# An attention and gated-MLP kernel: the last sum of x blocks cut in eight steps and set behind the bias additions

## The chip, the cores and the metric

The kernel runs on one core of a Trainium2 chip. The metric is device time in microseconds (us) of one execution; shown is the median of several.

## What is computed

Sigmoid attention for 8 batches of 12 heads, and behind it a gated MLP with a mixing over the sequence:

```python
# q, k, v: (8, 12, 448, 64);  S = 448, d_model = 768, d_ff = 1024
scores = scale * q @ k.T - log(S)
x = sigmoid(scores) @ v              # -> (8, 448, 768)
h = relu(x @ w_in)
u, v = h[..., :512], h[..., 512:]
v_n = (v - mean(v)) / sqrt(var(v) + 1e-6)
v_s = einsum('ts,bsd->btd', w_spatial, v_n) + b_spatial[None, :, None]
out = (u * v_s) @ w_out
```

## The kernel before

All data is float32. A matrix product is made of three products of rounded parts: each operand is kept as a high part and a low part (the rest), in the type fp32r. High parts are copies that ScalarE or VectorE makes, low parts are VectorE subtractions; `split` (lines 121 to 123) does both.

The program runs over four pairs of batches, m = 0 to 3. A pair goes through attention (scores psc, value products pav; x lands in `x_s`, high and low), then the MLP of the pair: `gate_values` (the half v of h: products pv, relu, layer norm into `mlp`) for the seven tiles of 128 rows in the groups (0, 1), (2, 3), (4, 5), (6,); then `spatial`, the mixing, in four blocks of 20 products into PSUM tiles pg, for the two batches b0, b1 and two pairs of feature blocks each; `biased`, which adds the bias to a finished pg on VectorE and puts the result g in SBUF (line 712; the fourth of them goes to `wval_s`); then the half u; then `output`.

For m = 1 to 3 the half u is made by `gated_by_blocks`: block products with seven instead of eight multiplications, as in Strassen's and Winograd's scheme. Blocks of the weights are ready sums in DRAM (`load_block` fetches them one by one on SyncE's queue, w_u_s<-w_u), and blocks of x are summed on VectorE: `x_sums` makes t2, t3 and t4 in a list of 21 steps (a generator, each `yield` one VectorE step, some with a ScalarE copy behind), `x_last_sum` makes t1 in place, in the parts of `x_s` that hold one block of x. `spare(n)` runs the next n steps of the lists in `jobs`, so the calls of `spare` in the layer norm and behind it fix where the steps stand. The seven products come in the order 11 (tiles ua), 21 (ub, first half), t2 (ua), t1 (ub, second half), t3 (ua), t4 (ua), 22 (ub). When 11 is done, ScalarE copies ua into the buffer r1; r1, r2, r3 are the results in SBUF.

PSUM has four buffers (pool ps_2, `bufs=4`) that rotate through pv, pg, ua, ub and po. The four pg take all of them; ua_m_0 takes the buffer of the first pg, ua_m_1 that of the second, ub_m_0 and ub_m_1 those of the third and fourth, each free when `biased` has read it.

At the end `in_program_order` chains each engine's instructions in the order in which the code wrote them, so each queue is fixed by the program text. Semaphores between engines are set by the tiles that instructions share.

Of the kernel before, what the change touches and what calls it, by code (L numbers as in the profile page):

```python
# [8 lines left out]
F32 = mybir.dt.float32  # L9
# [5 lines left out]
P = 128  # L15
# [20 lines left out]
def attn_gmlp_kernel(  # L36
# [25 lines left out]
    nc = tc.nc  # L62
    B, NHP, _, _ = qk.shape
    S = out.shape[3]
# [18 lines left out]
    work = ctx.enter_context(tc.tile_pool(name="work", bufs=2))  # L83
# [8 lines left out]
    KH = NCC // 2  # L92
# [9 lines left out]
    wval_s = const.tile([P, 3 * 512], U32, name="wval_s")  # L102
# [18 lines left out]
    def split(hi, lo, src, copy):  # L121
        copy(hi, src)  # L122
        nc.vector.tensor_sub(lo, src, hi.bitcast(F32))  # L123
# [304 lines left out]
    jobs = []  # L428

    def spare(n):  # L430

        while jobs and n:
            if next(jobs[0], None):
                n -= 1
            else:
                jobs.pop(0)
# [73 lines left out]
    sums = {}  # L510

    def x_part(k, j, ks, a):
        return x_s[:, a, k * KH + ks.start : k * KH + ks.stop, j * S : (j + 1) * S]
# [62 lines left out]

    def x_last_sum(m):

        ks = slice(0, KH)
        t = wval_s[:, : KH * S].bitcast(F32).rearrange("p (k s) -> p k s", k=KH)  # L580
        hi, lo = (x_part(0, 1, ks, a) for a in range(2))
        nc.vector.tensor_add(t, hi.bitcast(F32), lo.bitcast(F32))  # L582
        for a in range(2):
            nc.vector.tensor_sub(t, t, x_part(0, 0, ks, a).bitcast(F32))  # L584
        split(hi, lo, t, nc.scalar.copy)

    def gate_values(m, ts):

        n = len(ts)
        pv = banks(f"pv_{m}_{ts[0]}")  # L590
        for i, t in enumerate(ts):
            product(
                pv[:, i, :F],
                [
                    (
                        lambda a, cc=cc, t=t: x_s[:, a, cc, t * P : (t + 1) * P],
                        lambda c, cc=cc: w_g_s[:, cc, c, :],
                    )
                    for cc in range(NCC)
                ],  # L600
            )
        if n > 1:
            load_weights(1 if ts[0] else 5)
        if not ts[0]:
            spare(8)
        rv = work.tile([P, 2, 512], F32, tag="tmp", name=f"rv_{m}_{ts[0]}", bufs=3)
        nc.scalar.activation(rv[:, :n], pv[:, :n], AF.Relu)
        mv = work.tile([P, 2, 2], F32, tag="mv", name=f"mv_{m}_{ts[0]}")
        for i in range(n):
            stats = work.tile([P, 6], F32, tag="stats", name=f"stats_{m}_{ts[i]}")  # L610
            nc.vector.bn_stats(stats, rv[:, i])  # L611
            nc.vector.bn_aggr(mv[:, i], stats)
        rstd = work.tile([P, 2], F32, tag="rstd", name=f"rstd_{m}_{ts[0]}")
        mean = work.tile([P, 2], F32, tag="mean", name=f"mean_{m}_{ts[0]}")
        nc.gpsimd.tensor_scalar_add(rstd[:, :n], mv[:, :n, 1], 1e-6)
        nc.gpsimd.tensor_tensor(rstd[:, :n], rstd[:, :n], mhalf[:, :n], op=ALU.pow)
        if m:
            nc.vector.tensor_scalar_mul(mean[:, :n], mv[:, :n, 0], -1.0)
            spare(2)
        for i in range(n):  # L620
            if m:
                nc.scalar.activation(rv[:, i], rv[:, i], AF.Identity, bias=mean[:, i : i + 1])
            else:
                nc.vector.tensor_scalar_sub(rv[:, i], rv[:, i], mv[:, i, 0:1])
        load_weights(n - 1)
        for i, t in enumerate(ts):
            vn = slots["tile"][:, t]
            if t != NFULL:
                parts = [(vn[:, 0], vn[:, 1], slice(0, P))]
            else:  # L630

                a, c = slice(0, HALF), slice(HALF, P)
                parts = [(vn[a, 0], vn[c, 0], a), (vn[c, 1], vn[a, 1], c)]
            for hi, lo, rows in parts:
                if m:
                    nc.scalar.activation(  # L636
                        hi, rv[rows, i], AF.Identity, scale=rstd[rows, i : i + 1]
                    )
                else:
                    nc.vector.tensor_scalar_mul(hi, rv[rows, i], rstd[rows, i : i + 1])  # L640
                nc.vector.scalar_tensor_tensor(  # L641
                    lo,
                    rv[rows, i],
                    rstd[rows, i : i + 1],
                    hi.bitcast(F32),
                    op0=ALU.mult,
                    op1=ALU.subtract,
                )
            vns[t] = vn
        if n == 1:  # L650
            load_weights(1)
# [101 lines left out]
    def gated_by_blocks(m):  # L753

        b0, b1 = 2 * m, 2 * m + 1
        x = {
            name: [
                x_s[:, :, k * KH + ks, j * S : (j + 1) * S] for ks in range(KH)
            ]
            for name, k, j in (("11", 0, 0), ("21", 1, 0), ("22", 1, 1), ("t1", 0, 1))  # L760
        }
        x |= sums
        r1, r2 = (work.tile([P, 2, S], F32, tag="v", name=f"ur_{m}_{n}", bufs=2) for n in range(2))
        r3 = work.tile([P, 1024], F32, tag="raw", name=f"ur_{m}_2", bufs=4)[:, : 2 * S].rearrange(
            "p (i s) -> p i s", i=2
        )

        def products(ps, pos, mv, begins, then=None):
            w = block(pos)
            ops = [(a, ks, c) for ks in range(KH) for a, c in TERMS]  # L770
            for i in range(2):
                for n, (a, ks, c) in enumerate(ops):
                    col = (ks * 2 + i) * P
                    nc.tensor.matmul(  # L774
                        ps[i],
                        w[:, a, col : col + P],
                        x[mv][ks][:, c],
                        start=begins and n == 0,
                        stop=n == len(ops) - 1,
                        skip_group_check=True,  # L780
                    )
                if then:
                    then(i)
            if pos + SLOTS_U < NB:
                load_block(pos + SLOTS_U)

        def copied_to(r, ps):
            return lambda i: nc.scalar.copy(r[:, i], ps[i])

        def added_to(r, ps):  # L790
            return lambda i: nc.vector.tensor_add(r[:, i], ps[i], r[:, i])

        pairs = (0, 1), (2, 3)
        pa = [banks(f"ua_{m}_{i}")[:, 0, :S] for i in range(2)]
        products(pa, 0, "11", True, copied_to(r1, pa))
        both = [banks(f"ub_{m}_{i}") for i in range(2)]
        pw, pz = ([ps[:, n, :S] for ps in both] for n in range(2))
        products(pw, 1, "21", True, added_to(r1, pw))
        settle(b0, pairs[0], gates.pop((b0, pairs[0])), r1)
        products(pa, 2, "t2", False, copied_to(r2, pa))  # L800
        products(pz, 3, "t1", True)

        def copied_and_added(i):
            copied_to(r3, pa)(i)
            added_to(r3, pz)(i)

        products(pa, 4, "t3", False, copied_and_added)
        settle(b1, pairs[1], gates.pop((b1, pairs[1])), r3)
        products(pa, 5, "t4", False)
        g = gates.pop((b0, pairs[1]))  # L810
        settle(b0, pairs[1], g, [(g[:, i], pa[i]) for i in range(2)])
        products(pz, 6, "22", False, added_to(r2, pz))
        settle(b1, pairs[0], gates.pop((b1, pairs[0])), r2)
# [260 lines left out]
    for m in range(B // 2):  # L1074
        attention(m)
        slots_of_mlp(m)
        if m:
            jobs.append(x_sums(m))
        for ts in ((0, 1), (2, 3), (4, 5), (6,)):
            gate_values(m, ts)  # L1080
        if m:
            spare(99)
        b0, b1 = 2 * m, 2 * m + 1
        more = m < B // 2 - 1
        for b in (b0, b1):
# [4 lines left out]
        spatial_shorts(m, pairs)  # L1090
        biased(b0, pairs[0])
        if m:
            x_last_sum(m)
        for b, fcs in ((b0, pairs[1]), (b1, pairs[0])):
            spatial(b, fcs)
            biased(b, fcs)
        spatial(b1, pairs[1])
        if m:
            biased(b1, pairs[1])
            gated_by_blocks(m)  # L1100
            start_loads(m + 1)
            if more:
                for pos in range(SLOTS_U):
                    load_block(pos)
            output(b0, (0, 1))
        else:
            gated(b0, pairs[0])
            biased(b1, pairs[1])
            gated(b0, pairs[1])
            gated(b1, pairs[0])  # L1110
            start_loads(m + 1)
            output(b0, (0, 1))
            gated(b1, pairs[1])
            jobs.append(weight_sums())
# [72 lines left out]
```

## Time and profile before

| | |
|---|---|
| median of 3 runs | 664.58 us (662.57 to 664.81) |
| the profiled execution | 663.31 us, of which its span 661.5 us |
| TensorE (PE) busy | 649.5 us, 98% of the span |
| VectorE (DVE) busy | 398.7 us, 60% |
| ScalarE (ACT) busy | 311.1 us, 47% |
| GpSimd (POOL) busy | 27.8 us, 4% |
| mean granted TensorE clock | 0.995 of full |

The profile is of one execution; the span runs from its first to its last instruction. PE is TensorE's product, PEld its weight load, which overlaps it. A row of a timeline merges like instructions that follow each other ("x9") and says in brackets how long the engine stood idle ahead of it and what ended that. Ends of products are modelled, so starts are the safer numbers.

### The profile page before, as it was taken

The page shows a single profiled execution, that of the slowest core. Times are in us where ns is not written, and L with a number is a line of the kernel's source. Part 1 is how long each engine was busy: PE and PEld are TensorE (multiplying, and loading weights), DVE is VectorE, ACT ScalarE, POOL GpSimd, SP SyncE. Part 2 cuts the span into 40 slices and gives each one's busy share as a digit, 9 for nine tenths or more (in the row PEclk, how much of TensorE's full clock was granted, in tenths as well). Part 3 has the DMA queues.
Part 4 walks back from the last instruction along what each step waited for, and adds up shares of the span by engine and source line. Part 5 has one row for each costly group of instructions (what it writes and reads, how often), then busy time and mean ns, then how long its engine had stood idle before and what let it go on. Part 6 is the DMA issues. An engine that isn't in the chain of part 4 may idle for free.

```text
span 661.5 us, 10047 instructions
## 1 busy us (share of the span) xinstructions
PE 649.5 (98%) x4208; PEld 503.5 (76%) x4208; DVE 398.7 (60%) x549; ACT 311.1 (47%) x374; POOL 27.8 (4%) x63
## 2 busy tenths in 40 slices
PE   9999999999999999899999999989999999998997
PEld 3645889999765588799966658879996666887997
DVE  4989889849476386826066637673506754767420
ACT  6986322323777545122178745512218774541221
POOL 0000010000000002000000002100000000210000
PEclk9999999999999999999999999999999999999999
DMA  8764213565872000047544200003944410001213
GB/s 300 262 184 161 63 37 101 161 235 220 317 266 58 1 1 0 1 144 292 196 152 169 58 1 1 1 7 137 316 183 143 169 57 2 0 1 48 96 56 111
DMA packets 25117, 77.85 MB, mean 118 GB/s; under 512 B 2416, under 2 KB 8944, under 8 KB 25072
## 3 DMA queue, kind: packets, MB, share of 16 engines
q1 hardware_dynamic: 24784, 76.98, 33.5%
q8 instruction: 33, 0.54, 0.3%
q10 hardware_dynamic: 288, 0.23, 0.1%
q14 instruction: 12, 0.10, 0.1%
HBM read 60.69 MB, written 16.52 MB: 117 GB/s over the span
## 4 chain that ended last, share of the span: by engine, by line
PE 88%; DVE 8%; ACT 3%; issue 1%; POOL 1%; POOLq 0%
PE po L407 17%; PE pv L407 16%; PE pav L929 15%; PE psc L325 14%; PE ua L774 6%; PE ub L774 5%; PE pav L374 5%; PE pu L407 4%; PE psc L307 3%; PE pg L695 2%; DVE wval_s L584 1%; DVE mlp L641 1%; DVE g L712 1%; DVE stats L611 1%; DVE x_s L123 1%; DVE wval_s L582 1%
## 5 line engine op out<-in xcount | busy, mean ns | idle before, releaser
L407 PE MATMUL pv<-w_g_s,x_s 128*128 128x512 f32 x504 | 115.5, 390 | 0.0
L407 PEld LDWEIGHTS pv<-w_g_s,x_s 128*128 128x128 f32 x504 | 94.3, 188 | 22.3 <-issue 2.1
L289 ACT ACTIVATE ats<-psc,bias_s 128x896 f32<-128x896 f32 x102 | 95.1, 1006 | 19.9 <-PE pav L929 13.5
L325 PEld LDWEIGHTS psc<-qks 64*128 64x128 f32 x840 | 78.1, 185 | 14.8 <-issue 4.9
L325 PE MATMUL psc<-qks 64*128 64x448 f32 x840 | 88.6, 365 | 0.0
L407 PE MATMUL po<-mlp,w_out_s 128*128 128x448 f32 x396 | 82.8, 362 | 0.0
L407 PEld LDWEIGHTS po<-mlp,w_out_s 128*128 128x128 f32 x396 | 74.3, 188 | 4.9
L929 PE MATMUL pav<-ats,v 64*64 64x448 f32 x720 | 76.0, 539 | 0.0
L695 PE MATMUL pg<-w_sp_s,mlp 128*128 128x448 f32 x320 | 65.8, 364 | 0.0
L695 PEld LDWEIGHTS pg<-w_sp_s,mlp 128*128 128x128 f32 x320 | 59.7, 188 | 5.4 <-issue 1.2
L929 PEld LDWEIGHTS pav<-ats,v 64*64 64x64 f32 x720 | 28.3, 133 | 37.3 <-issue 26.6
L842 ACT COPY osb<-po 128x896 f32<-128x896 f32 x23 | 20.8, 906 | 65.2 <-PE po L407 62.1
L275 DVE TENSOR_TENSOR qks<-raw,qks 128x848 fp32r<-128x848 f32 x46 | 47.4, 1041 | 1.0
L123 DVE TENSOR_TENSOR x_s<-pav,x_s 128x896 fp32r<-128x896 f32 x16 | 17.4, 1090 | 50.8 <-ACT x_s L122 50.8
L407 PE MATMUL po<-gs,w_out_s 128*128 128x448 f32 x180 | 39.2, 362 | 0.0
L641 DVE SCALAR_TENSOR_TENSOR mlp<-rv,rstd,mlp 128x512 fp32r<-128x512 f32 (+1 forms) x32 | 23.5, 750 | 22.2 <-ACT mlp L636 21.7
L407 PEld LDWEIGHTS po<-gs,w_out_s 128*128 128x128 f32 x180 | 33.8, 188 | 2.3
L774 PE MATMUL ub<-x_s,w_u_s 128*128 128x448 f32 x162 | 35.4, 373 | 0.0
L268 DVE CAST qks<-raw 128x848 fp32r<-128x848 f32 x38 | 22.7, 597 | 19.3 <-PE po L407 13.1
L774 PEld LDWEIGHTS ub<-x_s,w_u_s 128*128 128x128 f32 x162 | 32.0, 197 | 2.4
L929 PE MATMUL pav<-at,v 64*64 64x448 f32 x216 | 31.9, 536 | 0.0
L901 DVE COPY wval_s<-psc 128x896 f32<-128x896 f32 x9 | 9.8, 1091 | 35.8 <-PE psc L325 35.8
(120 smaller groups left out, 794.4 us busy)
## 6 DMA issues: line engine op xcount, KB each, us to landing
raw<-qk_dram SPq DMA_DIRECT2D x47, 456.0 KB, 4.9
w_u_s<-w_u SPq DMA_DIRECT2D x21, 768.0 KB, 5.7
v<-v_dram SPq DMA_DIRECT2D x24, 448.0 KB, 3.4
out_dram<-osb SPq DMA_DIRECT2D x23, 448.0 KB, 2.6
wraw<-w_in_dram SPq DMA_DIRECT2D x12, 512.0 KB, 5.1
wraw<-w_out_dram SPq DMA_DIRECT2D x6, 512.0 KB, 3.8
w_u<-x_s SPq DMA_DIRECT2D x4, 768.0 KB, 3.6
w_u<-w_u_s SPq DMA_DIRECT2D x3, 768.0 KB, 5.6
```

The lines of the kernel that those rows point to most:

```text
L123: nc.vector.tensor_sub(lo, src, hi.bitcast(F32))
L268: (nc.vector.tensor_copy if b > 1 or halfway else nc.scalar.copy)(s[:, 0], raw)
L275: nc.vector.tensor_sub(s[:, 1], loaded[b, hp][:, HALF:], s[:, 0].bitcast(F32))
L289: nc.scalar.activation(at, src, AF.Sigmoid, bias=bias_s, scale=QK)
L325: nc.tensor.matmul(psc[:, j, :S], st[rows, k : k + P], mv[rows, Q:PART], start=i == 0, stop=i == len(ops) - 1,)
L374: nc.tensor.matmul(pav[heads, odd, :S], vt[rows, t, heads], at[rows, j], start=start, stop=t == NFULL,)
L407: nc.tensor.matmul(ps, st, mv, start=i == 0, stop=i == len(ops) - 1)
L641: nc.vector.scalar_tensor_tensor(lo, rv[rows, i], rstd[rows, i : i + 1], hi.bitcast(F32), op0=ALU.mult, op1=ALU.subtract,)
L695: nc.tensor.matmul(pg[:, i, :S], st, mv, start=n == 0 and not ended, stop=n == len(ops) - 1 and ended,)
L774: nc.tensor.matmul(ps[i], w[:, a, col : col + P], x[mv][ks][:, c], start=begins and n == 0, stop=n == len(ops) - 1, skip_group_check=True,)
L842: nc.scalar.copy(osb, po[:, :, :S])
L929: ins = nc.tensor.matmul(pavs[pair][heads, i % 2, :S], vt[rows, t if t == NFULL else t + i % 2 * (NFULL + 1), heads], at[rows, j], start=i ...
```

## The change

`x_last_sum` becomes a list of steps in `jobs` behind `x_sums`. It works in two halves, of two blocks (896 columns) and of one (448), each of one addition, two subtractions, a ScalarE copy of the high part, and a subtraction of the low part at the end: eight VectorE steps for four. Its scratch is r3 and the first part of r1 instead of `wval_s`; so r1, r2 and r3 are taken there and handed to `gated_by_blocks`. The call `spare(99)`, which ended the other sums ahead of the first bias, is gone; four steps run behind the first bias, three behind the second, three behind the third, the rest behind the fourth. And the layer norm of the tiles (2, 3) and (4, 5) takes three steps instead of two.

```diff
     def x_last_sum(m):
-        ks = slice(0, KH)
-        t = wval_s[:, : KH * S].bitcast(F32).rearrange("p (k s) -> p k s", k=KH)
-        hi, lo = (x_part(0, 1, ks, a) for a in range(2))
-        nc.vector.tensor_add(t, hi.bitcast(F32), lo.bitcast(F32))
-        for a in range(2):
-            nc.vector.tensor_sub(t, t, x_part(0, 0, ks, a).bitcast(F32))
-        split(hi, lo, t, nc.scalar.copy)
+        r3 = work.tile([P, 1024], F32, tag="raw", name=f"ur_{m}_2", bufs=4)[:, : 2 * S].rearrange(
+            "p (i s) -> p i s", i=2
+        )
+        r1, r2 = (work.tile([P, 2, S], F32, tag="v", name=f"ur_{m}_{n}", bufs=2) for n in range(2))
+        sums["r"] = r1, r2, r3
+        pending = []
+        for ks, t in ((slice(0, 2), r3), (slice(2, KH), r1[:, :1])):
+            hi, lo = (x_part(0, 1, ks, a) for a in range(2))
+            nc.vector.tensor_add(t, hi.bitcast(F32), lo.bitcast(F32))
+            yield True
+            nc.vector.tensor_sub(t, t, x_part(0, 0, ks, 0).bitcast(F32))
+            yield True
+            nc.vector.tensor_sub(t, t, x_part(0, 0, ks, 1).bitcast(F32))
+            nc.scalar.copy(hi, t)
+            yield True
+            pending.append((lo, t, hi.bitcast(F32)))
+        for op in pending:
+            nc.vector.tensor_sub(*op)
+            yield True
...
-            spare(2)
+            spare(3 if 0 < ts[0] and n > 1 else 2)
...
         if m:
-            jobs.append(x_sums(m))
+            jobs.extend([x_sums(m), x_last_sum(m)])
         for ts in ((0, 1), (2, 3), (4, 5), (6,)):
             gate_values(m, ts)
-        if m:
-            spare(99)
...
         biased(b0, pairs[0])
         if m:
-            x_last_sum(m)
+            spare(4)
         for b, fcs in ((b0, pairs[1]), (b1, pairs[0])):
             spatial(b, fcs)
             biased(b, fcs)
+            if m:
+                spare(3)
         spatial(b1, pairs[1])
         if m:
             biased(b1, pairs[1])
+            spare(99)
             gated_by_blocks(m)
```

Two places of the order, both of m = 1 (b0 = 2, b1 = 3); those of m = 2 and 3 are alike. Names: pg and g carry the batch and the first feature block of their pair, xt are the scratch tiles of the other sums, xs and x4 their results, ur_1_0 and ur_1_2 are r1 and r3.

VectorE, from the layer norm of tile 6 to the first addition of ub, before:

```order
L541 TENSOR_TENSOR xt_1_0_2097<-x_s_70 128x448
L544 TENSOR_TENSOR xs_1_1_2092<-xt_1_1_2098,xs_1_1_2092 128x448
L641 SCALAR_TENSOR_TENSOR mlp_1_2053<-rv_1_6_2273,rstd_1_6_2279,mlp_1_2053 128x512
...
L574 TENSOR_TENSOR x4_1_2_2096<-xt_1_1_2098,x4_1_2_2096 128x448
L712 TENSOR_TENSOR g_2_0_2328<-pg_2_0_2296,b_bc_73 128x2x448
L582 TENSOR_TENSOR wval_s_74<-x_s_70 128x1344
L584 TENSOR_TENSOR wval_s_74<-wval_s_74,x_s_70 128x1344 x2
L123 TENSOR_TENSOR x_s_70<-wval_s_74,x_s_70 128x3x448
L712 TENSOR_TENSOR g_2_2_2355<-pg_2_2_2317,b_bc_73 128x2x448
L712 TENSOR_TENSOR g_3_0_2377<-pg_3_0_2318,b_bc_73 128x2x448
L712 TENSOR_TENSOR wval_s_74<-pg_3_2_2319,b_bc_73 128x896
```

The same stretch after, from tile 6's last layer norm step on (L653 was L641, L724 was L712):

```order
L653 SCALAR_TENSOR_TENSOR mlp_1_2053<-rv_1_6_2275,rstd_1_6_2281,mlp_1_2053 128x512
L724 TENSOR_TENSOR g_2_0_2324<-pg_2_0_2292,b_bc_73 128x2x448
...
L587 TENSOR_TENSOR ur_1_2_2330<-x_s_70 128x896
L724 TENSOR_TENSOR g_2_2_2354<-pg_2_2_2313,b_bc_73 128x2x448
L589 TENSOR_TENSOR ur_1_2_2330<-ur_1_2_2330,x_s_70 128x896
L591 TENSOR_TENSOR ur_1_2_2330<-ur_1_2_2330,x_s_70 128x896
L587 TENSOR_TENSOR ur_1_0_2331<-x_s_70 128x448
L724 TENSOR_TENSOR g_3_0_2380<-pg_3_0_2314,b_bc_73 128x2x448
...
L596 TENSOR_TENSOR x_s_70<-ur_1_2_2330,x_s_70 128x2x448
L724 TENSOR_TENSOR wval_s_74<-pg_3_2_2315,b_bc_73 128x896
L596 TENSOR_TENSOR x_s_70<-ur_1_0_2331,x_s_70 128x448
```

The first bias addition moved from behind five steps of the other sums to right behind tile 6, and the other three stand between pieces of the last sum instead of behind it.

ScalarE at the same place, before:

```order
L607 ACTIVATE rv_1_6_2273<-pv_1_6_2254 128x512
L622 ACTIVATE rv_1_6_2273<-rv_1_6_2273,mean_1_6_2280 128x512
L636 ACTIVATE mlp_1_2053<-rv_1_6_2273,rstd_1_6_2279 128x512
L561 CAST xs_1_1_2092<-xt_1_1_2098 128x448
L570 CAST x4_1_2_2096<-xt_1_1_2098 128x448
L122 CAST x_s_70<-wval_s_74 128x3x448
L788 COPY ur_1_0_2400<-ua_1_0_2403 128x448
```

And after:

```order
L619 ACTIVATE rv_1_6_2275<-pv_1_6_2256 128x512
L561 CAST xs_1_1_2092<-xt_1_1_2098 128x448
L634 ACTIVATE rv_1_6_2275<-rv_1_6_2275,mean_1_6_2282 128x512
L648 ACTIVATE mlp_1_2053<-rv_1_6_2275,rstd_1_6_2281 128x512
L570 CAST x4_1_2_2096<-xt_1_1_2098 128x448
L592 CAST x_s_70<-ur_1_2_2330 128x2x448
L592 CAST x_s_70<-ur_1_0_2331 128x448
L797 COPY ur_1_0_2331<-ua_1_0_2408 128x448
```

One copy of the other sums moved ahead of tile 6's two activations, the copy of the last sum became two, and the copy of ua_1_0 now writes a buffer that the last sum has used.

## Rows read from the trace of the kernel before

**Rows 1.** The page: busy us of each engine, share of the span, instructions.

```profile
PE 649.5 (98%) x4208; PEld 503.5 (76%) x4208; DVE 398.7 (60%) x549; ACT 311.1 (47%) x374; POOL 27.8 (4%) x63
```

**Rows 2.** TensorE's waits: who waited for whom, us in all, times, longest.

```profile
PE ua L774 <- DVE g L712: 7.2, 3, 2.4
```

**Rows 3.** Timeline of TensorE: start, length, line, operation, idle before; m = 1, 2, 3.

```profile
262.34 12.28 PE L695 MATMUL pg<-w_sp_s,mlp 128*128 128x448 f32 x60
274.45 1.97 PE L774 MATMUL ua<-x_s,w_u_s 128*128 128x448 f32 x9
278.81 3.18 PE L774 MATMUL ua<-x_s,w_u_s 128*128 128x448 f32 x9 [2.39 <-DVE g L712]
281.79 4.30 PE L774 MATMUL ub<-x_s,w_u_s 128*128 128x448 f32 x18
...
437.77 1.97 PE L774 MATMUL ua<-x_s,w_u_s 128*128 128x448 f32 x9
442.11 2.72 PE L774 MATMUL ua<-x_s,w_u_s 128*128 128x448 f32 x9 [2.38 <-DVE g L712]
444.63 4.76 PE L774 MATMUL ub<-x_s,w_u_s 128*128 128x448 f32 x18
...
601.08 1.97 PE L774 MATMUL ua<-x_s,w_u_s 128*128 128x448 f32 x9
605.44 2.08 PE L774 MATMUL ua<-x_s,w_u_s 128*128 128x448 f32 x9 [2.40 <-DVE g L712]
607.36 3.76 PE L774 MATMUL ub<-x_s,w_u_s 128*128 128x448 f32 x18
```

**Rows 4.** Windows: length, TensorE busy (products), granted clock, DMA share, GB/s.

```profile
279.00:283.00 4.00, 4.00 (x13) 0.57 0.01 5
442.00:447.00 5.00, 4.89 (x16) 0.66 0.19 50
606.00:610.00 4.00, 4.00 (x22) 1.00 0.33 94
```

**Rows 5.** Timeline of VectorE and ScalarE in m = 1, tile 6 to fourth bias.

```profile
262.31 0.62 DVE L541 TENSOR_TENSOR xt<-x_s 128x448 f32<-128x448 f32 x1
...
262.49 0.72 ACT L622 ACTIVATE rv<-rv,mean 128x512 f32<-128x512 f32 x1 [1.46 <-DVE mean L618]
...
263.94 0.72 ACT L636 ACTIVATE mlp<-rv,rstd 128x512 fp32r<-128x512 f32 x1 [0.72 <-POOL rstd L616]
264.69 0.75 DVE L641 SCALAR_TENSOR_TENSOR mlp<-rv,rstd,mlp 128x512 fp32r<-128x512 f32 x1 [1.23 <-ACT mlp L636]
...
269.07 1.08 DVE L712 TENSOR_TENSOR g<-pg,b_bc 128x896 f32<-128x896 f32 x1
...
271.66 3.15 DVE L584 TENSOR_TENSOR wval_s<-wval_s,x_s 128x1344 f32<-128x1344 f32 x2
...
276.19 1.56 DVE L123 TENSOR_TENSOR x_s<-wval_s,x_s 128x1344 fp32r<-128x1344 f32 x1 [1.38 <-ACT x_s L122]
276.45 0.53 ACT L788 COPY ur<-ua 128x448 f32<-128x448 f32 x1 [0.29 <-PE ua L774]
277.67 2.08 DVE L712 TENSOR_TENSOR g<-pg,b_bc 128x896 f32<-128x896 f32 x2
...
279.67 1.08 DVE L712 TENSOR_TENSOR wval_s<-pg,b_bc 128x896 f32<-128x896 f32 x1
```

**Rows 6.** Groups by form, 228 to 305 us: count, busy, mean ns, idle before.

```profile
L541 DVE TENSOR_TENSOR xt<-x_s 128x896 f32<-128x896 f32 x4 | 4.3, 1087 | 0.1
...
L122 ACT CAST mlp<-g 128x896 fp32r<-128x896 f32 x1 | 0.9, 944 | 5.4 <-DVE g L740 5.4
...
L554 ACT CAST xs<-xt 128x448 fp32r<-128x448 f32 x1 | 0.6, 567 | 3.2 <-DVE xt L553 3.2
```

**Rows 7.** GpSimd's power by its line: ns min/median/max, first and last start.

```profile
L616 POOL TENSOR_TENSOR rstd<-rstd,mhalf x16: 578/933/1388, 77.6 to 589.7; 128x2 f32<-128x2 f32 x12, 128x1 f32<-128x1 f32 x4
```

**Rows 8.** DMA issues from 270 to 305 us: KB each, median us to landing.

```profile
w_u_s<-w_u SPq DMA_DIRECT2D x3, 768.0 KB, 4.2
```

More of the change, by code (lines that the diff above doesn't have):

```diff
@@ L761, in gated_by_blocks @@
         }
[L762 to L766, printed above, removed]
+        x |= {name: sums[name] for name in ("t2", "t3", "t4")}
+        r1, r2, r3 = sums.pop("r")
         def products(ps, pos, mv, begins, then=None):
```

## The prediction

> **What bounds the kernel now.** I read the page first: TensorE is busy for 98% of the span, while VectorE has 60% and ScalarE 47% [rows 1]. So only TensorE's gaps and slow stretches can be won, and a wait of the others counts only where it holds TensorE. The second view, TensorE's waits, names one place: ua's products wait for the bias addition g (L712), 7.2 us in three waits, one in each of the stages m = 1, 2, 3 [rows 2]. The third view, the timeline of TensorE, shows what such a wait costs altogether. In m = 1 the nine products of ua_1_0 begin at 274.45, those of ua_1_1 at 278.81, ub's at 281.79 [rows 3]. Undisturbed, a product of this shape takes 0.20 us: the 18 of ub in m = 3 take 3.76, of which 0.36 is the last one's own length, so 3.40 / 17 [rows 3]. Nine are 1.80. So from ua_1_0 to ua_1_1 2.56 us are lost, from ua_1_1 to ub 2.98 - 1.80 = 1.18, and in ub 4.30 - 3.76 = 0.54. The last two are no waits: between 279 and 283 us the granted clock is 0.57 of full, so for most of it 1.2 instead of 2.4 GHz [rows 4].
>
> The same for m = 2 (437.77, 442.11, 444.63, 4.76): 2.54 + 0.72 + 1.00, with a clock of 0.66 in 442 to 447. For m = 3 (601.08, 605.44, 607.36, 3.76): 2.56 + 0.12 + 0, with the clock at 1.00 [rows 3, 4]. So the waits lose 2.56 + 2.54 + 2.56 = 7.66 us, and the slow products behind them 1.72 + 1.72 + 0.12 = 3.56, together 11.22.
>
> Who is late is seen on VectorE's queue [rows 5]. PSUM has four buffers in rotation, all four held by pg tiles; ua_1_1 takes the second, free when the bias of (b0, second pair) has been added. The products of that tile were done by 266.4 (20 of the 60 from 262.34 on [rows 3]), but the addition starts at 277.67, since VectorE first ends the other sums, adds the first bias at 269.07, and then runs the last sum in four steps of some 1.56 with a wait of 1.38 for ScalarE's copy [rows 5].
>
> **The change, part by part.** *The last sum behind the biases.* Removed: four VectorE steps of 1344 columns, two in 3.15 and the others at 1.56, 6.27 us of work and 1.38 of waiting [rows 5], all ahead of three of the four biases. Added: four steps of 896 at 1.09 [rows 6] and four of 448 at 0.62 [rows 5], 6.84 us. So VectorE works 0.6 us more per stage; what it gains is the 1.38, and the order. TensorE, GpSimd and the DMA queue issue the same instructions in the same order.
>
> I follow VectorE's queue of m = 1, each step after the last with 0.04 between, which is cautious, as rows overlap where steps are independent (277.67 to 279.67 holds two additions of 1.08 in 2.08 [rows 5]). *Tile 6's gap* comes first: the step ahead of L641 is now L560, 262.31 to 262.93. Its ScalarE copy stands ahead of tile 6's two activations, so 262.97 to 263.54, at 0.57 as the like copy L554 takes [rows 6]; then L622 of 0.72 to 264.29. L636 began at 263.94 after waiting 0.72 for GpSimd [rows 5]; now it begins at 264.30, and L641 runs 0.36 later, 265.05 to 265.80. TensorE reaches tile 6 in the third block of spatial, 26 products behind 262.34, at 267.55: 1.75 us of cover, so this costs nothing.
>
> From there: first bias to 266.9; the three left of the other sums, with one copy between, to 269.5; first step of 896 to 270.6; **second bias to 271.8** (was 278.75); two steps of 896 and one of 448 to 274.7; **third bias to 275.8**; two of 448 and the pending low part of 896 to 278.25; **fourth bias to 279.4**; last low part to 280.0. Both ScalarE copies of the halves run under other VectorE steps: the 896 one (0.94 [rows 6]) from 274.1 to 275.0 is wanted at 277.2, the 448 one to 277.7 at 279.4. With the overlap of independent steps the fourth bias comes near 278.3.
>
> TensorE, without a wait from 274.45 on, wants ua_1_1's buffer at 276.25, ub's at 278.05 and 279.85, then ua again at 281.65, and the last sum itself (t1) at 285.25. Margins: 4.5, 2.2, **0.5 (to 1.5)**, and for t1 5.2. For ua at 281.65, ua_1_0 must have been copied into r1, which the last sum now uses as its scratch: ScalarE can start at 280.0 and ends at 280.6 (0.53 [rows 5]); 1.0 left. So every wait goes; next in line is the fourth bias.
>
> *One more step in the gaps* of tiles (2, 3) and (4, 5): 0.62 of VectorE each, while ScalarE has its activations; ScalarE's copy in (4, 5) comes earlier by one step. It is what leaves three of the other sums behind tile 6 instead of five. Cost none: TensorE wants tile 3 at 261.3 and tiles 4 and 5 at 266.4.
>
> *What starts earlier.* The load of weight block 4 follows the products of ua, so it moves forward with them; it lands in 4.2 us [rows 8], and is wanted 54 products, 10.8 us, later. The later work of the stage moves as one.
>
> **Sum.** 11.22 us against the profiled execution's own 663.31 (its span is 661.5, with 1.8 around it): **652.1 us**. That execution is 1.27 below the median. A third fall of the clock, in m = 3, would be 1.60 more and give 664.9, near the two slower runs, so the scatter may well be those falls (an estimate from rows 3); with the waits gone it goes too, and I leave the sum as it is. The bounds of this case: 0.9 below for scatter (the lowest run lies 0.74 under the profiled one), and up to 0.5 per stage, 653.6, if the fourth bias just misses.
>
> **The rivals.** *The clock falls anyway.* For it: one wait of 2.40 us, in m = 3, left the clock at 1.00 [rows 3, 4], so wait and fall are not one thing. Against: the two falls stand right behind such waits, and the page shows none elsewhere. Then only 7.66 come back: 655.7. The Trainium skill, "TensorE: Matmul & The Clock Gate", Part 1, says the half rate is the default which sustained activity lifts and idleness brings back; by that rule the full 11.22 return and this rival is empty, and two of the three waits here agree with it.
>
> *The wait moves to the fourth bias.* VectorE's queue is now full from tile 6 to the end, with 0.5 to 1.5 us to spare. If the two ScalarE waits that the rows of before show there (1.38 [rows 5], and about 0.6 behind a copy of 448) came in full, the fourth bias would end at 281.4, 1.5 late: 4.5 for three stages, and two falls of the clock (3.4): 660.0. If it is late by less, 654 to 660. Against: both copies have over a microsecond of other steps over them.
>
> *Slower: tile 6's layer norm slides, and the whole queue behind it.* L641 now stands ahead of everything, and waits for ScalarE (with a copy more) and GpSimd's power (L616), which takes 0.58 to 1.39 us [rows 7]. Each microsecond past 279.85 is one of TensorE's, plus 1.72 if the clock falls. A stage loses 3.74 now on average, so it turns slower once the fourth bias ends after 281.9, 2.5 behind my cautious sum; at 4 behind it a stage loses 5.3, in all 668.0. Against: GpSimd's whole spread is 0.81. The Trainium skill ("SBUF — State Buffer", Who interferes with whom) says that a VectorE instruction with two SBUF inputs and a GpSimd instruction that reads SBUF shut each other out for their whole length; by that an added step could hold L616 for 0.62 more, the fourth bias would be at 280.0, 0.2 late, and the sum 652.6, which no row settles.
>
> *The wait isn't the buffer's.* If something else released ua_1_1, nothing moves: 663.3. Against: TensorE restarts at 278.81 as the addition ends near 278.75, three times alike [rows 2, 3].
>
> **The numbers.** The forecast has 0.77; the clock 0.06; the fourth bias late 0.09, of which 0.04 is within 0.5% of before; slower 0.04; nothing moves 0.04. Under 0.5%, some 3.3 us, a measurement of this kernel cannot tell from no change. Faster 0.77 + 0.06 + 0.05 = 0.88, same 0.08, slower 0.04. The range reaches from 651.0 up over the clock's case to 656.3, and holds a little over 8 in 10.
>
> **What would show it.** Right: no wait of ua or ub on g; ua_m_0, ua_m_1, ub in one run of 36 products of about 7.4 us; granted clock 1.00 in all three places; second bias some 7 us earlier, the fourth 1 to 2.5 us earlier, against the start of ua. Wrong: ub waiting for wval_s's addition, ua's second use waiting for the copy into r1, spatial waiting for tile 6, or a slow stretch with no wait ahead of it.

## The result, and the profile after

| | before | after |
|---|---|---|
| median of 6 runs each | 663.72 us (661.14 to 664.81) | **652.39 us** (651.96 to 652.91) |
| ratio | | 0.9833, 95% interval 0.9813 to 0.9854 |
| the profiled execution, and its span | 663.31 us, 661.5 us | 652.91 us, 651.1 us |
| mean granted TensorE clock | 0.995 | 1.000 |

The forecast was 652.1 us, within 651.0 to 656.3. The page's first part and TensorE's list of waits, which answer to [rows 1] and [rows 2]:

```profile
PE 646.2 (99%) x4208; PEld 501.1 (77%) x4208; DVE 399.3 (61%) x561; ACT 311.4 (48%) x377; POOL 28.3 (4%) x63
...
PE warm L416 <- DVE ats L412: 1.2, 1, 1.2
```

The wait of ua for g is gone, and the only wait left is the one ahead of the warm-up at the program's start. VectorE is busy for 0.6 us more in all, and TensorE for 3.3 us less with the same 4208 products: that is about what the products at the lower clock lost in m = 1 and 2, 3.44 [rows 3, 4]. The timeline of TensorE, after, answers to [rows 3] (start, length, line, operation; L707 was L695, L783 was L774):

```profile
262.99 12.28 PE L707 MATMUL pg<-w_sp_s,mlp 128*128 128x448 f32 x60
275.11 3.77 PE L783 MATMUL ua<-x_s,w_u_s 128*128 128x448 f32 x18
278.71 3.76 PE L783 MATMUL ub<-x_s,w_u_s 128*128 128x448 f32 x18
...
434.16 3.77 PE L783 MATMUL ua<-x_s,w_u_s 128*128 128x448 f32 x18
437.76 3.76 PE L783 MATMUL ub<-x_s,w_u_s 128*128 128x448 f32 x18
...
593.30 3.77 PE L783 MATMUL ua<-x_s,w_u_s 128*128 128x448 f32 x18
596.91 3.76 PE L783 MATMUL ub<-x_s,w_u_s 128*128 128x448 f32 x18
```

Both halves of ua now merge into one row of 18, and ub follows 3.60 us later in every stage, which is 18 products at 0.20. The windows of the same places, as [rows 4] (length, TensorE busy, clock, DMA share, GB/s), have the clock at 1.00 and 22 products in 4 us where 13 stood:

```profile
279.00:283.00 4.00, 4.00 (x22) 1.00 0.57 197
437.00:441.00 4.00, 4.00 (x22) 1.00 0.43 152
597.00:601.00 4.00, 4.00 (x22) 1.00 0.56 197
```

The queue that was late, VectorE with ScalarE's pieces in m = 1, as [rows 5] (L653 was L641, L724 was L712, L797 was L788):

```profile
260.46 0.58 ACT L619 ACTIVATE rv<-pv 128x512 f32<-128x512 f32 x1
...
261.98 1.08 PE L682 MATMUL pg<-w_sp_s,mlp 64*128 64x448 f32 x8
...
265.01 0.75 DVE L653 SCALAR_TENSOR_TENSOR mlp<-rv,rstd,mlp 128x512 fp32r<-128x512 f32 x1 [1.42 <-ACT mlp L648]
265.68 1.08 DVE L724 TENSOR_TENSOR g<-pg,b_bc 128x896 f32<-128x896 f32 x1
...
270.13 1.08 DVE L724 TENSOR_TENSOR g<-pg,b_bc 128x896 f32<-128x896 f32 x1
...
273.80 1.08 DVE L724 TENSOR_TENSOR g<-pg,b_bc 128x896 f32<-128x896 f32 x1
...
276.99 1.08 DVE L724 TENSOR_TENSOR wval_s<-pg,b_bc 128x896 f32<-128x896 f32 x1
277.99 0.61 DVE L596 TENSOR_TENSOR x_s<-ur,x_s 128x448 fp32r<-128x448 f32 x1
...
278.68 0.97 ACT L797 COPY ur<-ua 128x448 f32<-128x448 f32 x2 [2.01 <-DVE x_s L596]
```

The four biases end at 266.8, 271.2, 274.9 and 278.1. Counted from the start of ua_1_0 (275.11), when the four buffers are wanted at 0, 1.8, 3.6 and 5.4 us, they are free 8.3, 5.7, 3.8 and 2.4 us ahead of that. The last step of the sum ends at 278.6, and only ScalarE's copy of ua_1_0 waits for it, at no cost.

### The profile page after: what moved, and what is told of

It is laid out like the page before. It is cut to its first block, busy times and chain, and to the rows that moved or that the text cites. A ratio compares the mean times of both kernels' runs of the same rounds, so it can differ in the third digit from the quotient of the medians.

```text
span 651.1 us, 10058 instructions
## 1 busy us (share of the span) xinstructions
PE 646.2 (99%) x4208; PEld 501.1 (77%) x4208; DVE 399.3 (61%) x561; ACT 311.4 (48%) x377; POOL 28.3 (4%) x63
## 4 chain that ended last, share of the span: by engine, by line
PE 99%; ACT 0%; DVE 0%; issue 0%
PE po L407 18%; PE pv L407 18%; PE pav L938 15%; PE psc L325 14%; PE pg L707 10%; PE ua L783 7%; PE pav L374 5%; PE ub L783 5%; PE pu L407 4%; PE psc L307 3%; PE pg L682 1%; PE warm L416 0%; ACT osb L846 0%; DVE ats L412 0%; DVE bias_s L104 0%
## 5 line engine op out<-in xcount | busy, mean ns | idle before, releaser
L707 PE MATMUL pg<-w_sp_s,mlp 128*128 128x448 f32 x320 | 65.8, 363 | 0.0
L707 PEld LDWEIGHTS pg<-w_sp_s,mlp 128*128 128x128 f32 x320 | 59.7, 187 | 5.4 <-issue 1.2
L653 DVE SCALAR_TENSOR_TENSOR mlp<-rv,rstd,mlp 128x512 fp32r<-128x512 f32 (+1 forms) x32 | 23.5, 750 | 17.4 <-ACT mlp L648 16.9
L783 PE MATMUL ub<-x_s,w_u_s 128*128 128x448 f32 x162 | 33.9, 362 | 0.0
L783 PEld LDWEIGHTS ub<-x_s,w_u_s 128*128 128x128 f32 x162 | 30.4, 187 | 2.0
```

What stands on the lines that cost most here:

```text
L653: nc.vector.scalar_tensor_tensor(lo, rv[rows, i], rstd[rows, i : i + 1], hi.bitcast(F32), op0=ALU.mult, op1=ALU.subtract,)
L707: nc.tensor.matmul(pg[:, i, :S], st, mv, start=n == 0 and not ended, stop=n == len(ops) - 1 and ended,)
L783: nc.tensor.matmul(ps[i], w[:, a, col : col + P], x[mv][ks][:, c], start=begins and n == 0, stop=n == len(ops) - 1, skip_group_check=True,)
```

## The experiments

All were made to tell three theories apart. The first is the prediction's: TensorE pays 1 us for each us by which VectorE's queue brings a bias after its place, and a wait brings slow products of its own behind it. The second: it is the cutting in halves that matters, not the place. The third: the clock falls for reasons of its own. For each run, "lost" is the time from the start of the group of products ahead of the wait to the start of the group that waited, less what the products between take at 0.20 us each, as the prediction counted it (the filling products are not taken off); m = 2 and 3 agree with m = 1 within 0.1 where only m = 1 is shown. The medians come from four comparisons, whose own medians of before were 663.72, 663.64, 663.46 and 664.34.

| run | buffer waited for | lost in m = 1 | 652.39 + 3 x lost | median measured |
|---|---|---|---|---|
| after | none | 0 | 652.4 | 652.39 |
| no extra step in the gaps | none | 0 | 652.4 | 652.43 |
| fourth bias 2.1 later | none | 0 | 652.4 | 652.27 |
| gap step alone | ua_1_1 | 0.95 | 655.2 | 655.41 |
| whole sum behind third bias | ub_1_1 | 1.16 | 655.9 | 655.80 |
| halves alone | ua_1_1 | 1.63 | 657.3 | 657.62 |
| whole sum behind second bias | ub_1_0 | 1.76 | 657.7 | 657.36 |
| before, wait filled (8 products) | ua_1_1 | 2.56 | 660.1 | 660.02 |
| before, wait filled (11 products) | ua_1_1 | 3.10 | 661.7 | 661.54 |
| before | ua_1_1 | 2.56 | 660.1 | 663.46 to 664.34 |
| fourth bias 5.5 later | ub_1_1 | 3.12 | 661.8 | 666.33 |

The first row sets the sum; eight others follow the place alone, within 0.4 us. Only the two in which TensorE stands idle for 2.4 us or more lie above it, by 3.4 to 4.5 us. The runs one by one:

**The place alone, behind the second and behind the third bias.** The sum stays whole, in `wval_s`, with no extra step in the gaps.

```diff
         biased(b0, pairs[0])
-        if m:
-            x_last_sum(m)
         for b, fcs in ((b0, pairs[1]), (b1, pairs[0])):
             spatial(b, fcs)
             biased(b, fcs)
+            if m and b == b0:   # the other run: b == b1
+                x_last_sum(m)
```

> The last sum stays whole (four steps of 1344, scratch wval_s, no extra step in the gaps) and moves as one piece from behind the first bias addition to behind the second. My theory, that TensorE loses what VectorE's queue puts ahead of the bias it waits for: the second bias ends near 271.2 in m = 1, the third waits for the whole sum and ends near 279.8, 1.7 after ub's first half wants its buffer. So the wait moves from ua to ub, about 1.7 to 1.9 a stage, 5.4 us above the changed kernel: 657.8, up to 661 with the clock falling behind it. Rival, that cutting the sum in halves is what matters: no gain, 663.7 as before.

The timeline of this run (657.36 us; ratio to before 0.9914, 0.9893 to 0.9934): two biases in a row, then the third behind the sum, and ub waits for it.

```profile
268.80 2.08 DVE L712 TENSOR_TENSOR g<-pg,b_bc 128x896 f32<-128x896 f32 x2
...
274.17 3.77 PE L774 MATMUL ua<-x_s,w_u_s 128*128 128x448 f32 x18
...
278.39 1.08 DVE L712 TENSOR_TENSOR g<-pg,b_bc 128x896 f32<-128x896 f32 x1
...
279.53 3.88 PE L774 MATMUL ub<-x_s,w_u_s 128*128 128x448 f32 x18 [1.60 <-DVE g L712]
```

> The whole sum moves behind the third bias addition. My theory: the fourth ends near 280.8 in m = 1, 1.0 after ub's second half wants its buffer: 1.0 to 1.2 a stage, 655.6, up to 659 with falls of the clock. Rival, that the halves matter: 663.7. The step from the run behind the second bias to this one should be about 0.7 us a stage.

Measured 655.80 (ratio 0.9891, 0.9867 to 0.9915), and the wait has moved on to the second half of ub:

```profile
277.82 1.96 PE L774 MATMUL ub<-x_s,w_u_s 128*128 128x448 f32 x9
...
279.63 1.09 DVE L712 TENSOR_TENSOR wval_s<-pg,b_bc 128x896 f32<-128x896 f32 x1
...
280.78 2.08 PE L774 MATMUL ub<-x_s,w_u_s 128*128 128x448 f32 x9 [0.99 <-DVE wval_s L712]
```

Moving one undivided piece by two places brings some 8 of the 11 us. That speaks against the second theory; the place alone is worth most of the gain, and the waits are near what the queue said. The step between the two runs is 0.6 us a stage by the starts and 0.5 by the medians, where I had expected 0.7.

**The halves alone.** The new `x_last_sum`, with all its steps at the old place, and two steps in the gaps.

```diff
...
         biased(b0, pairs[0])
         if m:
-            x_last_sum(m)
+            jobs.append(x_last_sum(m))
+            spare(99)
```

> The sum is cut in eight steps with the new scratch, but all eight stand where the four stood, between the first and the second bias, and the gaps of the layer norm have two steps as before. My theory: only the 1.38 of waiting for ScalarE's copy goes and 0.2 to 0.6 of work comes, so the second bias ends about 1.2 earlier (277.6) and ua still waits, 1.2 to 1.4 a stage: 656 to 660. Rival, that the halves matter and not the place: 652.4.

Measured 657.62 (ratio 0.9917, 0.9896 to 0.9937). The second bias starts 0.93 earlier than in [rows 5], as no wait for ScalarE is left on VectorE's way:

```profile
274.45 1.97 PE L783 MATMUL ua<-x_s,w_u_s 128*128 128x448 f32 x9
...
276.74 2.08 DVE L724 TENSOR_TENSOR g<-pg,b_bc 128x896 f32<-128x896 f32 x2
...
277.88 2.08 PE L783 MATMUL ua<-x_s,w_u_s 128*128 128x448 f32 x9 [1.46 <-DVE g L724]
```

So halving alone, too, brings 6.0 us (663.64 in this comparison): some 2.8 by the shorter wait (three times 2.56 - 1.63), the rest by the clock, which stayed at 1.00 behind all three waits. It works as the place does, by what stands ahead of the second bias, and the 652.4 of the second theory is not reached.

**The gap step alone, and all but the gap step.** One line, in the kernel before (first run) and taken back from the changed one (second).

```diff
-            spare(2)
+            spare(3 if 0 < ts[0] and n > 1 else 2)
```

> Only the third step in the gaps of tiles (2, 3) and (4, 5); the last sum stays whole behind the first bias, as before. My theory: three of the other sums stand ahead of the first bias instead of five, less the 0.32 by which tile 6's last step is later, so the second bias comes 0.9 earlier and the wait of ua is 1.5 instead of 2.4 a stage: 657 to 661. Rival, that the extra step gives nothing or costs time in the layer norm: 663.7 or more.

Measured 655.41 (ratio 0.9885, 0.9864 to 0.9906), better than I expected by 1.6 us and more. The timeline shows why:

```profile
261.87 12.28 PE L695 MATMUL pg<-w_sp_s,mlp 128*128 128x448 f32 x60
...
263.89 0.75 DVE L641 SCALAR_TENSOR_TENSOR mlp<-rv,rstd,mlp 128x512 fp32r<-128x512 f32 x1 [1.42 <-ACT mlp L636]
...
273.99 1.97 PE L774 MATMUL ua<-x_s,w_u_s 128*128 128x448 f32 x9
...
275.60 2.08 DVE L712 TENSOR_TENSOR g<-pg,b_bc 128x896 f32<-128x896 f32 x2
...
276.74 2.08 PE L774 MATMUL ua<-x_s,w_u_s 128*128 128x448 f32 x9 [0.79 <-DVE g L712]
```

Tile 6's last step L641 starts 2.02 us behind the 60 products of spatial, where it started 2.35 behind them before (264.69 and 262.34 [rows 3, 5]). I had put it 0.32 later instead of 0.33 earlier, so the second bias gains 1.6 us and not 0.9; and the clock stayed at 1.00 behind the three waits of 0.8.

> The changed kernel with two steps instead of three in the gaps of tiles (2, 3) and (4, 5); all else as changed. My theory: the two steps go to the end of the list, behind the fourth bias, all biases stay in time, and nothing moves: 652.4, no wait of TensorE. Rival, that the extra step is a part of the gain: above 653.5, with a wait of ua or ub.

Measured 652.43 (ratio 0.9827, 0.98 to 0.9855), with no wait of ua or ub. With the other parts in place the step is worth nothing; alone it is worth some 8 us. Each part of this change alone brings half of the gain or more. That the whole gain comes without one of them was run for the gap step only; the kernel with the sum undivided and all else changed was not run.

**How much room is left.** Additions of 896 columns into r2, which is not read before it is written anew, stand ahead of the fourth bias of the changed kernel; two in the first run, five in the second.

```diff
         if m:
+            for _ in range(2):   # the other run: 5
+                nc.vector.tensor_add(
+                    sums["r"][1], *(x_part(1, 0, slice(0, 2), i).bitcast(F32) for i in range(2))
+                )
             biased(b1, pairs[1])
```

> The changed kernel with two additional additions of 896 columns on VectorE (into r2, which nobody reads before it is written anew) ahead of the fourth bias in m = 1 to 3, some 2.1 us. In the trace of the changed kernel that bias ends at 278.07 and ub's second half wants its buffer near 280.5, so there are 2.4 to spare: 652.4, at most 653. The rival of the prediction, that VectorE's queue is full (0.5 to spare): 1.6 a stage, 657.

Measured 652.27 (ratio 0.9826, 0.9798 to 0.9854). The fourth bias ends at 279.97, and the second half of ub runs on without a break from 278.48:

```profile
276.76 2.21 DVE L1109 TENSOR_TENSOR ur<-x_s 128x896 f32<-128x896 f32 x2
...
278.48 3.76 PE L783 MATMUL ub<-x_s,w_u_s 128*128 128x448 f32 x18
...
278.89 1.08 DVE L724 TENSOR_TENSOR wval_s<-pg,b_bc 128x896 f32<-128x896 f32 x1
```

> The same with five additional additions, some 5.1 us. The fourth bias ends near 283.2, 2.7 after it is wanted, a wait of about 2.8 a stage: 8.4 us above the changed kernel, 660.8, and up to 5.2 more if the clock falls behind each wait: 660.8 to 666. If the wait stood for nothing but the queue, exactly 1 us for each us past the point.

Measured 666.33 (ratio 1.0041, 1.0025 to 1.0056), slower than the kernel before and 0.3 above what I expected. The fourth bias starts at 282.46, so five additions bring it 5.5 us later against the start of ua_1_0, not 5.1; the timeline of TensorE and the windows behind the three waits:

```profile
278.68 1.96 PE L783 MATMUL ub<-x_s,w_u_s 128*128 128x448 f32 x9
283.60 2.51 PE L783 MATMUL ub<-x_s,w_u_s 128*128 128x448 f32 x9 [2.95 <-DVE wval_s L724]
285.90 4.96 PE L783 MATMUL ua<-xs,w_u_s 128*128 128x448 f32 x18
290.69 1.56 PE L783 MATMUL ub<-x_s,w_u_s 128*128 128x448 f32 x7
```

```profile
285.00:289.00 4.00, 4.00 (x14) 0.57 0.46 131
449.00:453.00 4.00, 4.00 (x14) 0.59 0.48 144
613.00:617.00 4.00, 4.00 (x14) 0.61 0.51 160
```

The clock fell behind each of the three waits. In m = 1 that costs (285.90 - 283.60 - 1.80) + (290.69 - 285.90 - 3.60) = 1.69 us, near the 1.72 of [rows 3, 4]. So this is the prediction's slower rival, brought about by the additions: with two of them it does not come, with five it does; three and four were not run.

**The wait without idling.** In the kernel before, products into the second half of ua_m_0's PSUM tile, which nobody reads, stand between those of ua_m_0 and ua_m_1; eleven in the first run, eight in the second.

```diff
                 if then:
                     then(i)
+                if pos == 0 and i == 0:
+                    for _ in range(11):   # the other run: 8
+                        nc.tensor.matmul(
+                            uas[0][:, 1, :S], w[:, 0, :P], x[mv][0][:, 0],
+                            start=True, stop=True, skip_group_check=True,
+                        )
...
-        pa = [banks(f"ua_{m}_{i}")[:, 0, :S] for i in range(2)]
+        uas = [banks(f"ua_{m}_{i}") for i in range(2)]
+        pa = [ps[:, 0, :S] for ps in uas]
```

> The kernel before, with eleven products (2.2 us) between those of ua_1_0 and ua_1_1 that fill the wait; they write the second half of ua_1_0's PSUM tile, which nobody reads. The wait for the bias stays, but TensorE is busy in it. My theory, that the slow products behind the waits are the idle time's own: the clock stays at 1.00, the loss is the 7.66 of the place alone, 652.1 + 7.7 = 659.8, and the runs lie within 1 us of each other. Rival, that the clock falls for another reason: slow stretches stay, 661 to 665.

Measured 661.54 (ratio 0.9968, 0.9953 to 0.9983; 660.97 to 661.88 in 10 runs). The clock held, at 1.00 in the 10 us from ua_m_0 on in all three stages; the time is 1.7 us above what I expected, since eleven were too many:

```profile
274.31 1.97 PE L774 MATMUL ua<-x_s,w_u_s 128*128 128x448 f32 x9
...
276.89 2.48 PE L786 MATMUL ua<-x_s,w_u_s 128*128 128x448 f32 x11 [0.62 <-ACT ur L798]
...
279.21 1.96 PE L774 MATMUL ua<-x_s,w_u_s 128*128 128x448 f32 x9
```

The filling also waited for ScalarE's copy of the tile's first half, and ended after the bias (277.51 + 1.08 = 278.6). Hence the second run:

> The kernel before with eight filling products instead of eleven. With eleven, the filling began 0.62 late, since it also waited for ScalarE's copy of ua_1_0, and ended 0.6 after the bias, so that ua_1_1 began 3.10 us after its place instead of 2.56. Eight end near 278.5 in m = 1, as the bias does: 2.55 a stage, 7.7 in all, the clock at 1.00: 652.4 + 7.7 = 660.1, runs within 1 us. Rival, that the filling itself costs something else: 661.5 again.

Measured 660.02 (ratio 0.9938, 0.9922 to 0.9954; 659.4 to 660.79 in 7 runs):

```profile
274.33 1.97 PE L774 MATMUL ua<-x_s,w_u_s 128*128 128x448 f32 x9
276.92 1.88 PE L786 MATMUL ua<-x_s,w_u_s 128*128 128x448 f32 x8 [0.62 <-ACT ur L798]
278.69 2.08 PE L774 MATMUL ua<-x_s,w_u_s 128*128 128x448 f32 x9
...
274.00:284.00 10.00, 9.38 (x47) 1.00 0.20 71
```

ua_1_1 starts 4.36 us behind ua_1_0, as it did before (278.81 - 274.45 [rows 3]); the wait is as long, and 24 useless products are added, yet the kernel is 4.3 us faster than before in the same comparison (664.34), because the products behind run at the full clock (1.00 in all three stages). That rules out the third theory: with 0.62 us of idling instead of 2.39, and nothing else of the wait changed, the clock does not fall. The two terms of the prediction's sum are so measured apart: 660.02 - 652.39 = 7.6 us for the waits, and for the clock 4.3 in the same comparison, or 3.4 against the 663.46 of the runs of before in the other one.

## Why the prediction was right, and where its sizes were off

**The sum.** 7.66 for the waits (measured 7.6) and 3.56 for the slow products (3.4 to 4.3, by which runs of before one compares with) made 11.22; the medians differ by 11.33, the spans of the two profiled executions by 10.4. The span after starts with a delay ahead of everything that the change touches: its first short scores start at 26.56 instead of 26.05, and at the start of the first block of spatial in m = 1 it is 0.66 late. From the start of the first block of spatial in m = 1 to the end it is 661.5 - 257.22 = 404.28 before and 651.1 - 257.88 = 393.22 after, 11.06 less.

**The scatter.** I took the scatter of the runs of before for a number of clock falls, as an estimate. In the 19 runs that stood beside the second group of experiments, time and mean granted clock go in steps: 661.18 to 662.37 at 0.997 (4 runs), 663.35 to 663.53 at 0.995 (6), 664.18 to 665.65 at 0.992 (8), and one of 662.93 at 0.994. The three groups have means of 661.6, 663.4 and 664.7; one, two and three falls would fit this, but only the profiled runs show falls themselves: two in before (0.995), three in the run with five additions (0.991). All six runs after are at 1.000 and within 1 us, as the prediction let the scatter go with the waits. It took base and slow products from the same profiled execution, so that sum needed no luck with the number of falls.

**Tile 6's layer norm was mis-sized.** The prediction let L641 run 0.36 later against TensorE. Against the start of the 60 products it is 265.01 - 262.99 = 2.02 now, 2.35 before: 0.33 earlier. I had noted that ScalarE's copy in the gap of (4, 5) moves one step forward, but did not carry it on: all that stands behind it on ScalarE, down to the relu of tile 6, moves too. That relu starts at 260.46 in both traces, but TensorE's short products, 261.98 now, stood at 261.32 before; so it is 0.66 earlier against TensorE. Without the gap step (all else changed) the distance is 2.35 again, 265.11 - 262.76, and with the gap step alone it is 2.02. The two places before:

```profile
260.46 0.58 ACT L607 ACTIVATE rv<-pv 128x512 f32<-128x512 f32 x1
...
261.32 1.09 PE L670 MATMUL pg<-w_sp_s,mlp 64*128 64x448 f32 x8
```

**So the margin of the fourth bias was 2.4 us, not 0.5 to 1.5.** It ends 2.96 after the start of ua_1_0; my cautious walk said 4.95, the one with overlap 3.85. Of the 2.0 between, 0.7 is tile 6, the rest that each independent step starts 0.08 before the one ahead has ended, instead of 0.04 behind it (270.13, 271.13). So against the start of ua_1_0 the second bias ends 8.2 us earlier than before, and the fourth 3.3, more than the 7 and the 1 to 2.5 that were to show the forecast right. The overlap also fits with VectorE being busy for 0.6 us more in all, where the prediction had 0.6 in each stage. All these errors lay on the safe side. The rival "the wait moves to the fourth bias" was therefore further off than its margin of 0.5 to 1.5 made it look: with 2.1 us added ahead of that bias no wait appears.

**The clock's rival** (0.06) is settled by the filled wait, and by the kernel after, which has no slow stretch in the three places. The rule of the Trainium skill, "TensorE: Matmul & The Clock Gate", Part 1, that full rate is what sustained activity gives and idleness takes away, agrees with the 1.00 of all three windows after and with both filled runs. Why the wait of 2.40 us in m = 3 of before left the clock at 1.00 [rows 3, 4] stays open.

**The slower rival** was sized rightly in its price, 1 us for each us past the point (3.12 lost where the fourth bias ended 3.06 late) and 1.7 a stage for the clock; but it counted from a margin of 0.5 where there were 2.4. GpSimd's power takes 1.06 us in the gap of (4, 5) both before and after, although a VectorE step more runs beside it after; in tile 6's gap, which has two VectorE steps in both kernels, it takes 0.93 instead of 0.80. The Trainium skill ("SBUF — State Buffer", Who interferes with whom) has a VectorE instruction with two SBUF inputs contend with a GpSimd instruction that reads SBUF; the 0.62 more that the prediction drew from this shows in neither gap.

## What to carry to other kernels

Where an engine hands back buffers to the bound engine, count each hand-back against the moment at which that buffer is wanted, and move what is wanted later behind it; here each of four edits alone brought half of the gain or more. When a step moves, follow the engine that works behind it as well: the copy that went one place forward shifted all of the next tile's activations. And price a wait of the bound engine with what comes behind it: 7.6 us of waiting cost 11 here.

## What the runs showed of the hardware that was not expected

What a wait cost in clock differed with its length. Behind waits of 0.8 to 1.6 us (four kernels, three waits each) the granted clock stayed at 1.00 in the profiled runs, and all sixteen runs have a mean of 0.999 or 1.000. Behind 2.4 us it fell in two stages of three in the profiled run of before; the steps of the mean clock suggest one to three falls by run. Behind 2.95 us the profiled run shows three falls, and nine of ten runs have a mean clock of 0.991 or 0.992. No run has a wait between 1.6 and 2.4 us, and the waits also stand at different buffers, so the runs do not show what decides.

And a wait filled with products that compute nothing made the kernel faster: by 4.3 us of 664 with eight products a stage, and by 1.9 with eleven, in the comparison of each.
